# Two PSUM pools of four banks, another order of loads and of batch 0's work, and one two-term weight chunk in a fused attention and maxout kernel

## The chip, the cores and the metric

The kernel runs on one core of a Trainium2 chip. The metric is the time of one execution on the device in microseconds (us); lower is better. TensorE (PE in the profile, PEld for its weight loads) does the matmuls, VectorE (DVE), ScalarE (ACT) and GpSimd (POOL) do the casts, sums and copies, and SyncE's queue (SP) issues nearly all DMAs. Matmul results go to PSUM, which the kernel uses in banks of 128 x 512 fp32.

## The reference

```python
B, H, S, Ns, D = (8, 8, 512, 32, 64)          # n_tokens of the second part: B * (S + Ns)
scores = scale * x @ state.T ; a = softmax(scores)        # [B,H,S,Ns]
xread = a @ state                                         # [B,H,S,D]
scores2 = scale * state @ x.T ; a2 = softmax(scores2)
sread = a2 @ x                                            # [B,H,Ns,D]
t = concat([xread, sread], axis=2) -> [B * (S + Ns), H * D] = [4352, 512]
h1 = t @ w1 ; h2 = t @ w2                                 # d_ff = 1024
out = maximum(h1, h2) @ w_out                             # [4352, 512]
```

All inputs and the output are float32 in HBM.

## The kernel before, in words

**Algebra.** max(h1, h2) is h2 + relu(h1 - h2), so the kernel needs W1 - W2 (`wcat`, columns 0 to 1023) and W2 @ W_out (`wcat`, columns 1024 to 1535, made by `w_wo`). xread is a @ state, so for each batch the small matrix S W = blockdiag(state) @ wcat (`SW`, made by `u_sw` in chunks of 512 columns) takes the place of xread @ W. A batch of 512 tokens is then a first layer `l1` (eight tiles: a @ SW, then relu into `r`) and a second layer `l2` (four output tiles `c`: two matmuls for the linear part, eight for relu @ W_out).

**One batch's preparation.** `compact_x` (ScalarE) casts x to `xc`, `d_xt` transposes it by DMA to `xt`; `u_exp` makes the scores and their exponentials `e`; `u_norm` the row sums `es`, reciprocals `er` and products `a`; `d_at` transposes `a` by DMA to `aT` (in batches 0 and 1 `u_at` does it on TensorE). `u_sr` (lines 235 to 249) reads the same `e` for the other direction: 32 matmuls into one bank, from which VectorE takes a reciprocal `rr` and a product `sr`; `u_srt` transposes that into `sread_t`. `u_sw` (lines 275 to 291) puts out the matmuls of all its chunks first, two banks for each, and then their copies: VectorE takes g=0, ScalarE g=1.

**Order.** The schedule is written by hand: instructions go to each engine's queue in the order of the program, and each engine works its queue in order. For batches 1 to 7 (lines 522 to 533) `fillers(b)` hangs the preparation of batch b+1 between the tiles of batch b: the scores after the last first-layer tile (slot 7), `u_sr` and the compaction of x(b+2) after output tile 0 (slot 8), `d_at` after tile 1 (slot 9), `u_sw` with all three chunks after tile 2 (slot 10), `u_srt` after tile 3 (slot 11). Output tiles 0 and 2 are copied from PSUM by VectorE, 1 and 3 by ScalarE (`l2_close`). For batch 0 and the making of weights the order is spelled out in lines 443 to 520, with warm-up matmuls in the gaps.

**PSUM.** Until batch 0 is done there are two pools of four banks, `ps` for short-lived tiles and `acc` for output tiles and W2 @ W_out. `one_ring` (line 521) then closes both, and one ring of eight banks serves everything. A new tile takes a bank only when the readers of its last tile are done.

**Two terms.** W1 - W2 is made by GpSimd (`w_sub`, four parts). Chunks of `SW` that are wanted sooner, (0,0), (0,1) and (1,1) as (batch, chunk), are made in two terms instead: state @ bf16(W1) plus (-state) @ bf16(W2), with `w1b`, `w2b` and `sneg`.

**Loads.** SP issues, in this order: states of batches 0 to 2, x(0), W2 left half, W_out quarters 0 and 1, W2 right half, W_out quarters 2 and 3, W1 left and right half, x(1), states of batches 3 to 7, x(2).

Of the kernel before, what the change touches and what calls it, by code (L numbers as in the profile page):

```python
# [9 lines left out]
BF16 = mybir.dt.bfloat16  # L10
# [5 lines left out]
def kernel(  # L16
# [14 lines left out]
    nc = tc.nc  # L31
# [6 lines left out]
    NF = FF // 128  # L38
    scale = 1.0 / (D ** 0.5)
    assert D == 64 and Ns == 32 and S == 512 and H == 8 and DM == 512 and B % 4 == 0  # L40
    TWO = 2
    WC = FF + DM

    consts = ctx.enter_context(tc.tile_pool(name="consts", bufs=1))
# [3 lines left out]
    keep = ctx.enter_context(tc.tile_pool(name="keep", bufs=2))  # L48
    big = ctx.enter_context(tc.tile_pool(name="big", bufs=2))

    early = ctx.enter_context(ExitStack())
    pools = dict(ps=early.enter_context(tc.tile_pool(name="ps", bufs=4, space=bass.MemoryType.PSUM)),
                 acc=early.enter_context(tc.tile_pool(name="acc", bufs=4, space=bass.MemoryType.PSUM)))
    ctx.enter_context(tc.manual_schedule())

    def bank(dtype=F32, kind="ps"):
        return pools[kind].tile([128, 512 if dtype == F32 else 1024], dtype, tag="b", name=kind)

    def acc():
        return bank(kind="acc")  # L60

    def one_ring():
        early.close()
        pools["ps"] = pools["acc"] = ctx.enter_context(tc.tile_pool(name="ring", bufs=8, space=bass.MemoryType.PSUM))

    def copy(eng, o, i):
        if eng == "A":
            nc.scalar.copy(o, i)  # L68
        elif eng == "V":
            nc.vector.tensor_copy(o, i)  # L70
        else:
            nc.gpsimd.tensor_copy(o, i)  # L72

    def negate(eng, o, i):
        (nc.vector if eng == "V" else nc.gpsimd).tensor_scalar(o, i, scalar1=-1.0, scalar2=None, op0=ALU.mult)
# [8 lines left out]
    def load_x(b, parts=1):  # L84
        xf_t[b] = xio.tile([128, H, NC * D], F32, tag="xf", name="xf")
        for g in range(parts):
            nc.sync.dma_start(out=xf_t[b][:, g::parts, :], in_=x[b, g::parts].rearrange("h (p c) d -> p h (c d)", c=NC))
# [3 lines left out]
    def load_states(bs):  # L91
        nc.sync.dma_start(out=s_f[:, 2 * bs.start:2 * bs.stop],
                          in_=state[bs].rearrange("b (q h) n d -> (h n) (b q) d", q=2))

    first, rest = slice(0, 3), slice(3, 8)
    w2f = stage.tile([128, 4, FF], F32)
    w1f = stage.tile([128, 4, FF], F32)
    wof = stage.tile([128, NF, DM], F32)
# [1 line left out]
    def load_w(t, w, ch):  # L100
        cs = slice(ch * 512, (ch + 1) * 512)
        nc.sync.dma_start(out=t[:, :, cs], in_=w.rearrange("(i p) f -> p i f", p=128)[:, :, cs])  # L102
# [3 lines left out]
                          in_=moe_w_out.rearrange("(k p) n -> p k n", p=128)[:, 2 * q:2 * q + 2])  # L106

    load_states(first)
    load_x(0)
    for ch in range(2):  # L110
        load_w(w2f, moe_w2, ch)
        load_wo(2 * ch)
        load_wo(2 * ch + 1)
    load_w(w1f, moe_w1, 0)
    load_w(w1f, moe_w1, 1)
    load_x(1)
    load_states(slice(3, 8))
    load_x(2)

    ident = consts.tile([128, 128], BF16)  # L120
# [2 lines left out]
    make_identity(nc, ident)  # L123
    sbd = consts.tile([128, B, H, 2, Ns], BF16)
    nc.vector.memset(sbd, 0.0)
    sneg = consts.tile([128, TWO, 4, Ns], BF16)
    wo = consts.tile([128, NF, DM], BF16)
    wcat = consts.tile([128, 4, WC], BF16)
    w1b = stage.tile([128, 4, FF], BF16)
    w2b = stage.tile([128, 4, FF], BF16)  # L130
    w2t = stage.tile([128, 4, NF, 128], BF16)

    def warm_up(n):
        p = bank()
        for k in range(n):
            nc.tensor.matmul(p, warm[:, 0:128], warm, start=(k == 0), stop=(k == n - 1))  # L136
# [28 lines left out]
    def negate_states():  # L165
        for g in range(2):
            gs = slice(64 * g, 64 * g + 64)
            negate("V", sneg[gs], sbd[gs, 0:TWO, g::2, g, :])


    sread_t = consts.tile([128, 4, B * Ns], BF16)
# [63 lines left out]
    def u_sr(b):  # L235

        d = st[b]
        d["sr"] = at.tile([128, 2, D], BF16, tag="sr", name="sr")
        d["rr"] = at.tile([128, 2], F32, tag="rr", name="rr")
        p = bank()  # L240
        for g in range(2):
            for c in range(NC):
                for i in range(4):
                    nc.tensor.matmul(p[32 * i:32 * i + 32, g * 65:g * 65 + 65], d["e"][:, g, i, c, :],  # L244
                                     d["xp"][:, 2 * i + g, c, 0:65],
                                     start=(c == 0 and g == 0), stop=(c == NC - 1 and g == 1))
        pv = p[:, 0:130].rearrange("p (g u) -> p g u", g=2)
        nc.vector.reciprocal(d["rr"], p[:, 64:130:65])
        nc.vector.tensor_mul(d["sr"], pv[:, :, 0:64], d["rr"].unsqueeze(2).to_broadcast([128, 2, D]))
# [23 lines left out]
    swt = consts.tile([128, 2, 2, WC], BF16)  # L273

    def sw_mm(b, ch, engs="VA"):
        pg = [bank(), bank()]
        two = b < TWO and ch < 2 and (b, ch) != (1, 0)
        terms = ((sbd, w1b), (sneg, w2b)) if two else ((sbd, wcat),)
        for k, (sv, w) in enumerate(terms):
            for i in range(4):  # L280
                for g in range(2):
                    gs = slice(64 * g, 64 * g + 64)
                    nc.tensor.matmul(pg[g][32 * i:32 * i + 32, :],  # L283
                                     sneg[gs, b, i, :] if k else sbd[gs, b, 2 * i + g, g, :],
                                     w[gs, i, ch * 512:(ch + 1) * 512],
                                     start=(k == 0), stop=(k == len(terms) - 1))
        return lambda: [copy(engs[g], SW[b][:, g, ch * 512:(ch + 1) * 512], pg[g]) for g in range(2)]

    def u_sw(b, *chs):
        for out_of in [sw_mm(b, ch) for ch in chs]:  # L290
            out_of()
# [92 lines left out]
                nc.sync.dma_start(out=out[b * L + S:(b + 1) * L], in_=ob[32 * q:32 * q + 32, t, :])  # L384


    def w_sub(q):
        cs = slice(q * 256, (q + 1) * 256)
        nc.gpsimd.tensor_sub(wcat[:, :, cs], w1f[:, :, cs], w2f[:, :, cs])  # L389

    def w_cast(o, w, ch, engs="VA"):
        cs = slice(ch * 512, (ch + 1) * 512)
        for k in range(2):
            copy(engs[k], o[:, 2 * k:2 * k + 2, cs], w[:, 2 * k:2 * k + 2, cs])
# [16 lines left out]
    def w_wo(q, i):  # L411
        if q == 0:
            WO[i] = acc()
        for f in range(2 * q, 2 * q + 2):
            nc.tensor.matmul(WO[i], w2t[:, i, f, :], wo[:, f, :], start=(f == 0), stop=(f == NF - 1))  # L415
        if q == 3:
            copy("V" if i % 2 else "A", wcat[:, i, FF:WC], WO[i])


    def fillers(b):  # L420
        fill = {}

        def put(slot, *units):
            fill.setdefault(slot, []).extend(units)

        n = b + 1
        if n < B:
            put(7, lambda: u_sc(n, 0), lambda: u_sc(n, 1))
            put(8, lambda: u_sr(n))
        if n + 1 < B:  # L430
            put(8, lambda: compact_x(n + 1, 0), lambda: compact_x(n + 1, 1))
        if n < B:
            put(9, lambda: d_at(n))
            put(10, lambda: u_sw(n, 0, 1, 2))
        if n + 1 < B:
            put(10, lambda: d_xt(n + 1))
        if n < B:
            put(11, lambda: u_srt(n))
        return fill
# [3 lines left out]
    warm_up(6)  # L443
    cast_states("V", first)
    states(first)
    warm_up(5)
    cast_x(0, (("V", slice(0, 4, 2)), ("A", slice(4, 8, 2)), ("V", slice(1, 4, 2)), ("P", slice(5, 8, 2))))
    u_xt(0, 0, "V")
    u_xt(0, 1, "A")
    u_exp(0, 0)  # L450
    u_exp(0, 1)
    w_cast(w2b, w2f, 0, "VV")
    wo_cast(0, "P")
    wo_cast(1, "P")
    warm_up(1)
    w_t(0, 0, "A")
    w_t(0, 1, "A")
    u_norm(0, 0, nc.vector)
    u_sr(0)
    u_norm(0, 1, nc.vector)  # L460
    negate_states()
    warm_up(3)
    for q in range(2):
        for i in range(4):
            w_wo(q, i)
    w_cast(w2b, w2f, 1)
    wo_cast(2, "P")
    w_t(1, 0, "V")
    w_t(1, 1, "A")
    u_at(0, "V")  # L470
    u_srt(0)
    wo_cast(3, "V")
    for i in range(4):
        w_wo(2, i)
    w_cast(w1b, w1f, 0)
    w_sub(0)
    w_sub(1)
    for i in range(4):
        w_wo(3, i)
    u_sw(0, 0)  # L480
    u_sw(0, 2)
    l1(0, {}, range(0, 4))
    for c in range(NC):
        l2_open(0, c)
    w_cast(w1b, w1f, 1)
    compact_x(1, 0)
    compact_x(1, 1)
    d_xt(1)
    cast_x(1)
    w_sub(2)  # L490
    w_sub(3)
    cast_states("P", rest)
    load_x(3)
    sT = d_states(rest)
    l2_add(0, 0, range(0, 4))
    u_sw(0, 1)
    for c in range(1, NC):
        l2_add(0, c, range(0, 4))
    l1(0, {}, range(4, 8))
    u_sc(1, 0, nc.vector)  # L500
    u_sc(1, 1, nc.gpsimd)
    cast_x(2)
    l2_add(0, 0, range(4, 8))
    l2_close(0, 0)
    u_sw(1, 0)
    l2_add(0, 1, range(4, 8))
    l2_close(0, 1)
    u_sw(1, 1)
    u_sr(1)
    compact_x(2, 0)  # L510
    compact_x(2, 1)
    l2_add(0, 2, range(4, 8))
    l2_close(0, 2)
    u_at(1, "V")
    l2_add(0, 3, range(4, 8))
    l2_close(0, 3)
    d_xt(2)
    u_sw(1, 2)
    u_srt(1)
    l2_out(0)  # L520
    one_ring()
    for b in range(1, B):
        fill = fillers(b)
        if b + 2 < B:
# [39 lines left out]
```

The softmax here doesn't subtract the row's maximum and nothing guards it: scores larger than these inputs give would overflow.

## Time and profile before

| | |
|---|---|
| median of 8 runs | 152.27 us (151.82 to 153.05) |
| profiled execution | 152.10 us, span from first to last instruction 150.2 us |
| TensorE busy | 141.9 us (94%) |
| VectorE, ScalarE, GpSimd busy | 82.3, 75.7, 43.9 us |
| DMA | 29.89 MB, 199 GB/s over the span; 364 to 390 GB/s from 4 to 23 us |
| TensorE clock granted | 0.988 of full speed |
| first matmul of batch 1's first layer | 42.04 us |
| one batch from there (batches 1 to 6) | 13.96 us |

How to read it: a row of the timeline gives the start, the time from the first start to the last end, the engine, the line of the kernel, the operation, `out<-in`, and how often; a square bracket holds the idle time ahead of it and what ended that. Matmuls overlap: a 128x512 matmul is shown with 0.379 us, and the next starts 0.216 us after it. Rows of the chain of waits hold a start, a duration and what ran or was waited for; "issue" is time without a cause that the profile shows.

### The profile page before, as it was taken

How to read it: one execution, taken by the hardware profiler on the slowest of the kernel's cores; microseconds unless marked ns; L12 is line 12 of the kernel's file. 1: busy time of each engine (PE TensorE's matmuls, PEld its weight loads, DVE VectorE, ACT ScalarE, POOL GpSimd, SP SyncE). 2: the span in 40 equal slices, each digit the busy share in tenths (PEclk: the TensorE clock that was granted, in tenths of full speed). 3: DMA queues.
4: the chain of work that ended last, by engine and by line, in shares of the span. 5: the costliest groups of instructions: out<-in, count | busy, mean ns of one | idle time of the engine just before them, and what ended most of it. 6: DMA issues, size and time to landing. Idle time of an engine off the chain costs nothing.

```text
span 150.2 us, 3032 instructions
## 1 busy us (share of the span) xinstructions
PE 141.9 (94%) x1255; PEld 68.1 (45%) x1255; DVE 82.3 (55%) x151; ACT 75.7 (50%) x126; POOL 43.9 (29%) x44
## 2 busy tenths in 40 slices
PE   6859999999989999999999999999999999999990
PEld 1347553343435445444543444345445434764460
DVE  5368558428968187716854583658067725721120
ACT  3057239926869147717744683478157136521000
POOL 3025129995843430550064017104100500000000
PEclk9987999999999999999999999999999999999999
DMA  4999999988699877974979397951596030502423
GB/s 87 365 390 387 388 385 334 300 164 248 124 257 299 226 132 236 313 147 79 293 266 195 123 283 222 149 232 61 105 111 279 0 74 35 244 0 70 140 105 110
DMA packets 37934, 29.89 MB, mean 199 GB/s; under 512 B 24864, under 2 KB 33312, under 8 KB 37024
## 3 DMA queue, kind: packets, MB, share of 16 engines
q1 hardware_dynamic: 37776, 29.56, 70.1%
q8 instruction: 10, 0.16, 0.5%
q10 hardware_dynamic: 144, 0.13, 0.3%
q14 instruction: 4, 0.03, 0.1%
HBM read 15.20 MB, written 8.91 MB: 161 GB/s over the span
## 4 chain that ended last, share of the span: by engine, by line
PE 71%; DMA 13%; SPq 8%; ACT 3%; DVE 2%; issue 1%
PE acc L326 32%; PE ps L311 16%; DMA xf<-in_x_dram 10%; PE acc L322 9%; SPq L102 4%; SPq L105 3%; PE ps L283 3%; DMA xt<-xc 3%; PE ps L370 2%; PE acc L380 2%; PE ps L221 2%; PE acc L360 1%; PE ps L244 1%; ACT xc L68 1%; PE acc L378 1%; DVE es L228 1%
## 5 line engine op out<-in xcount | busy, mean ns | idle before, releaser
L326 PE MATMUL acc<-wo,r 128*128 128x512 bf16 x248 | 58.9, 379 | 0.0
L326 PEld LDWEIGHTS <-r 128*128 128x128 bf16 x248 | 23.9, 98 | 28.8 <-issue 0.6
L301 DVE TENSOR_SCALAR r<-ps 128x512 bf16<-128x512 f32 x32 | 22.1, 692 | 16.2 <-PE ps L311 16.1
L311 PE MATMUL ps<-aT,swt 128*128 128x512 bf16 x128 | 29.1, 379 | 0.9 <-ACT sread_t L68 0.8
L231 POOL TENSOR_TENSOR a<-e,er 128x512 bf16<-128x512 bf16 x13 | 13.4, 1048 | 54.2 <-ACT e L224 27.2
L70 DVE COPY ob<-acc 128x512 f32<-128x512 f32 (+1 forms) x17 | 11.1, 653 | 30.1 <-PE acc L326 29.7
L68 ACT COPY ob<-acc 128x512 f32<-128x512 f32 (+1 forms) x16 | 9.2, 573 | 28.6 <-PE acc L326 21.0
L299 ACT ACTIVATE r<-ps 128x512 bf16<-128x512 f32 x32 | 19.2, 601 | 8.3 <-PE ps L311 7.7
L68 ACT CAST swt<-ps 128x512 bf16<-128x512 f32 x24 | 12.9, 593 | 12.3 <-PE ps L283 12.2
L311 PEld LDWEIGHTS <-swt 128*128 128x128 bf16 x128 | 12.1, 98 | 15.3 <-DVE swt L70 1.3
L322 PE MATMUL acc<-swt,aT 128*128 128x512 bf16 x62 | 18.1, 381 | 0.0
L72 POOL CAST xp<-xf 128x2048 bf16<-128x2048 f32 (+1 forms) x8 | 14.1, 1768 | 10.6 <-DMA xf<-in_x_dram 10.6
L70 DVE CAST swt<-ps 128x512 bf16<-128x512 f32 x24 | 15.3, 682 | 1.7 <-PE ps L283 1.7
L68 ACT CAST xc<-xf 128x1024 bf16<-128x1024 f32 x14 | 14.0, 1051 | 0.1
L228 DVE TENSOR_REDUCE es<-e 128x16 f32<-128x512 bf16 x16 | 10.6, 662 | 1.8 <-ACT e L224 1.8
L389 POOL TENSOR_TENSOR wcat<-w1f,w2f 128x1024 bf16<-128x1024 f32 x4 | 9.8, 2475 | 2.9 <-DMA w1f<-in_moe_w_dram 2.9
L224 ACT ACTIVATE e<-ps 128x512 bf16<-128x512 f32 x16 | 8.8, 595 | 1.3 <-PE ps L221 0.6
L136 PE MATMUL ps<-warm 128*128 128x512 bf16 x15 | 6.3, 568 | 1.3 <-POOL warm L122 1.3
L322 PEld LDWEIGHTS <-aT 128*128 128x128 bf16 x62 | 4.7, 98 | 6.0 <-issue 2.6
L415 PE MATMUL acc<-wo,w2t 128*128 128x512 bf16 x32 | 7.2, 379 | 0.0
L283 PE MATMUL ps<-wcat,sbd 64*32 64x512 bf16 x168 | 6.7, 380 | 0.1
L221 PEld LDWEIGHTS <-xt 128*128 128x128 bf16 x128 | 5.0, 101 | 2.9 <-ACT xt L68 0.7
(68 smaller groups left out, 104.4 us busy)
## 6 DMA issues: line engine op xcount, KB each, us to landing
xf<-in_x_dram SPq DMA_DIRECT2D x8, 1024.0 KB, 7.6
out_dram<-ob SPq DMA_DIRECT2D x7, 1024.0 KB, 5.0
w2f<-in_moe_w_dram SPq DMA_DIRECT2D x2, 1024.0 KB, 10.4
wof<-in_moe_w_out_dram SPq DMA_DIRECT2D x4, 512.0 KB, 11.4
w1f<-in_moe_w_dram SPq DMA_DIRECT2D x2, 1024.0 KB, 15.0
out_dram<-ob SPq DMA_DIRECT2D x3, 256.0 KB, 2.7
out_dram<-obs SPq DMA_DIRECT2D x8, 64.0 KB, 1.7
s_f<-in_state_dram SPq DMA_DIRECT2D x1, 320.0 KB, 13.7
```

The source lines that it names most:

```text
L68: nc.scalar.copy(o, i)
L70: nc.vector.tensor_copy(o, i)
L72: nc.gpsimd.tensor_copy(o, i)
L228: nc.vector.tensor_reduce(d["es"][:, g], d["e"][:, g].rearrange("p i c n -> p (i c) n"), axis=mybir.AxisListType.X, op=ALU.add)
L231: mul.tensor_mul(d["a"][:, g].rearrange("p c i n -> p i c n"), d["e"][:, g], d["er"][:, g].rearrange("p (i c) -> p i c", i=4).unsqueeze(3) ...
L283: nc.tensor.matmul(pg[g][32 * i:32 * i + 32, :], sneg[gs, b, i, :] if k else sbd[gs, b, 2 * i + g, g, :], w[gs, i, ch * 512:(ch + 1) * 512 ...
L299: nc.scalar.activation(out=o, in_=p, func=ACTF.Relu)
L301: nc.vector.tensor_scalar(o, p, scalar1=0.0, scalar2=None, op0=ALU.max)
L311: nc.tensor.matmul(p, SW[b][:, g, f * 128:(f + 1) * 128], AT[b][:, g, :], start=(g == 0), stop=(g == 1))
L322: nc.tensor.matmul(OB[b][1 + c], AT[b][:, g, c * 128:(c + 1) * 128], SW[b][:, g, FF:WC], start=(g == 0), stop=False)
L326: nc.tensor.matmul(OB[b][1 + c], R[b][:, f, c * 128:(c + 1) * 128], wo[:, f, :], start=False, stop=(f == NF - 1))
L389: nc.gpsimd.tensor_sub(wcat[:, :, cs], w1f[:, :, cs], w2f[:, :, cs])
```

## The change

It does these things at once:

- The two PSUM pools of four banks stay for the whole kernel. `u_sw` takes `acc` banks for its third chunk from batch 2 on, `ps` banks otherwise.
- In the steady loop `u_sr(n)` goes from slot 8 to slot 10, directly ahead of `u_sw(n)`.
- Only chunk (0,0) has two terms. `w_sub` parts 2 and 3 go from GpSimd to VectorE, `w1b` has half the columns and is cast in three parts by VectorE, ScalarE and GpSimd.
- States of batch 0 alone lead the queue of loads; those of batches 1 and 2 come just before x(1), are cast by GpSimd and transposed on TensorE within batch 0's second layer. x(0) is loaded in two halves (even and odd heads).
- Early casts go to other engines, and there are 25 warm-up matmuls instead of 15.
- Batch 0's second layer: `u_sw(1,0)` moves ahead of the scores of batch 1, both of batch 1's products `a` go to GpSimd, and three of the four copies of output tiles move behind the last tile.

```diff
-    early = ctx.enter_context(ExitStack())
-    pools = dict(ps=early.enter_context(tc.tile_pool(name="ps", bufs=4, space=bass.MemoryType.PSUM)),
-                 acc=early.enter_context(tc.tile_pool(name="acc", bufs=4, space=bass.MemoryType.PSUM)))
+    pools = {k: ctx.enter_context(tc.tile_pool(name=k, bufs=4, space=bass.MemoryType.PSUM)) for k in ("ps", "acc")}
...
-    first, rest = slice(0, 3), slice(3, 8)
+    first, second, rest = slice(0, 1), slice(1, 3), slice(3, 8)
...
     load_states(first)
-    load_x(0)
+    load_x(0, 2)
...
     load_w(w1f, moe_w1, 1)
+    load_states(second)
     load_x(1)
...
     def sw_mm(b, ch, engs="VA"):
-        pg = [bank(), bank()]
-        two = b < TWO and ch < 2 and (b, ch) != (1, 0)
+        pg = [bank(kind="acc" if ch == 2 and b > 1 else "ps") for g in range(2)]
+        two = (b, ch) == (0, 0)
...
-    def w_sub(q):
+    def w_sub(q, eng=nc.gpsimd):
         cs = slice(q * 256, (q + 1) * 256)
-        nc.gpsimd.tensor_sub(wcat[:, :, cs], w1f[:, :, cs], w2f[:, :, cs])
+        eng.tensor_sub(wcat[:, :, cs], w1f[:, :, cs], w2f[:, :, cs])
...
             put(7, lambda: u_sc(n, 0), lambda: u_sc(n, 1))
-            put(8, lambda: u_sr(n))
...
-            put(10, lambda: u_sw(n, 0, 1, 2))
+            put(10, lambda: u_sr(n), lambda: u_sw(n, 0, 1, 2))
...
-    warm_up(5)
-    cast_x(0, (("V", slice(0, 4, 2)), ("A", slice(4, 8, 2)), ("V", slice(1, 4, 2)), ("P", slice(5, 8, 2))))
+    warm_up(9)
+    cast_x(0, (("A", slice(0, 4, 2)), ("V", slice(4, 8, 2)), ("P", slice(1, 4, 2)), ("V", slice(5, 8, 2))))
...
-    w_cast(w2b, w2f, 0, "VV")
+    w_cast(w2b, w2f, 0, "PA")
...
-    w_cast(w1b, w1f, 0)
+    for e, i in (("V", slice(0, 2)), ("A", slice(2, 3)), ("P", slice(3, 4))):
+        copy(e, w1b[:, i, 0:512], w1f[:, i, 0:512])
...
     l1(0, {}, range(0, 4))
-    for c in range(NC):
-        l2_open(0, c)
-    w_cast(w1b, w1f, 1)
+    w_sub(2, nc.vector)
+    w_sub(3, nc.vector)
     compact_x(1, 0)
     compact_x(1, 1)
     d_xt(1)
+    cast_states("P", second)
+    cast_states("P", rest)
     cast_x(1)
-    w_sub(2)
-    w_sub(3)
-    cast_states("P", rest)
     load_x(3)
     sT = d_states(rest)
+    for c in range(NC):
+        l2_open(0, c)
     l2_add(0, 0, range(0, 4))
+    l2_add(0, 1, range(0, 4))
+    states(second)
+    l2_add(0, 2, range(0, 4))
     u_sw(0, 1)
-    for c in range(1, NC):
-        l2_add(0, c, range(0, 4))
+    l2_add(0, 3, range(0, 4))
     l1(0, {}, range(4, 8))
-    u_sc(1, 0, nc.vector)
-    u_sc(1, 1, nc.gpsimd)
+    u_sw(1, 0)
+    u_exp(1, 0)
+    u_exp(1, 1)
+    u_norm(1, 0, nc.gpsimd)
+    u_norm(1, 1, nc.gpsimd)
     cast_x(2)
     l2_add(0, 0, range(4, 8))
-    l2_close(0, 0)
-    u_sw(1, 0)
+    u_sw(1, 1)
+    u_sr(1)
     l2_add(0, 1, range(4, 8))
     l2_close(0, 1)
-    u_sw(1, 1)
-    u_sr(1)
     compact_x(2, 0)
     compact_x(2, 1)
+    d_xt(2)
     l2_add(0, 2, range(4, 8))
-    l2_close(0, 2)
+    u_sw(1, 2)
     u_at(1, "V")
-    l2_add(0, 3, range(4, 8))
-    l2_close(0, 3)
-    d_xt(2)
-    u_sw(1, 2)
+    l2_add(0, 3, range(4, 6))
     u_srt(1)
+    l2_add(0, 3, range(6, 8))
+    for c in (3, 0, 2):
+        l2_close(0, c)
     l2_out(0)
-    one_ring()
```

More of the change, by code (lines that the diff above doesn't have):

```diff
@@ L40 @@
     assert D == 64 and Ns == 32 and S == 512 and H == 8 and DM == 512 and B % 4 == 0
-    TWO = 2
     WC = FF + DM
@@ L60, in acc @@
         return bank(kind="acc")
-    def one_ring():
-        early.close()
-        pools["ps"] = pools["acc"] = ctx.enter_context(tc.tile_pool(name="ring", bufs=8, space=bass.MemoryType.PSUM))
     def copy(eng, o, i):
@@ L115 @@
     load_w(w1f, moe_w1, 1)
+    load_states(second)
     load_x(1)
-    load_states(slice(3, 8))
+    load_states(rest)
     load_x(2)
@@ L125 @@
     nc.vector.memset(sbd, 0.0)
-    sneg = consts.tile([128, TWO, 4, Ns], BF16)
+    sneg = consts.tile([128, 4, Ns], BF16)
     wo = consts.tile([128, NF, DM], BF16)
     wcat = consts.tile([128, 4, WC], BF16)
-    w1b = stage.tile([128, 4, FF], BF16)
+    w1b = stage.tile([128, 4, 512], BF16)
     w2b = stage.tile([128, 4, FF], BF16)
@@ L167, in negate_states @@
             gs = slice(64 * g, 64 * g + 64)
-            negate("V", sneg[gs], sbd[gs, 0:TWO, g::2, g, :])
+            negate("V", sneg[gs], sbd[gs, 0, g::2, g, :])
     sread_t = consts.tile([128, 4, B * Ns], BF16)
@@ L283, in sw_mm @@
                     nc.tensor.matmul(pg[g][32 * i:32 * i + 32, :],
-                                     sneg[gs, b, i, :] if k else sbd[gs, b, 2 * i + g, g, :],
+                                     sneg[gs, i, :] if k else sbd[gs, b, 2 * i + g, g, :],
                                      w[gs, i, ch * 512:(ch + 1) * 512],
@@ L415, in w_wo, with w_wo_out @@
             nc.tensor.matmul(WO[i], w2t[:, i, f, :], wo[:, f, :], start=(f == 0), stop=(f == NF - 1))
-        if q == 3:
-            copy("V" if i % 2 else "A", wcat[:, i, FF:WC], WO[i])
+    def w_wo_out(i):
+        copy("V" if i % 2 else "A", wcat[:, i, FF:WC], WO[i])
     def fillers(b):
@@ L445 @@
     states(first)
-    warm_up(5)
-    cast_x(0, (("V", slice(0, 4, 2)), ("A", slice(4, 8, 2)), ("V", slice(1, 4, 2)), ("P", slice(5, 8, 2))))
+    warm_up(9)
+    cast_x(0, (("A", slice(0, 4, 2)), ("V", slice(4, 8, 2)), ("P", slice(1, 4, 2)), ("V", slice(5, 8, 2))))
     u_xt(0, 0, "V")
+    warm_up(2)
     u_xt(0, 1, "A")
     u_exp(0, 0)
+    warm_up(2)
     u_exp(0, 1)
-    w_cast(w2b, w2f, 0, "VV")
+    warm_up(3)
+    w_cast(w2b, w2f, 0, "PA")
+    u_norm(0, 0, nc.vector)
+    u_norm(0, 1, nc.vector)
+    w_t(0, 0, "A")
+    w_t(0, 1, "A")
+    u_sr(0)
     wo_cast(0, "P")
@@ L455 @@
     warm_up(1)
[L456 to L465, printed above, removed]
+    for i in range(4):
+        w_wo(0, i)
+    u_at(0, "V")
     w_cast(w2b, w2f, 1)
-    wo_cast(2, "P")
+    for i in range(4):
+        w_wo(1, i)
     w_t(1, 0, "V")
     w_t(1, 1, "A")
-    u_at(0, "V")
+    negate_states()
+    wo_cast(2, "P")
+    wo_cast(3, "P")
     u_srt(0)
-    wo_cast(3, "V")
+    warm_up(2)
     for i in range(4):
         w_wo(2, i)
-    w_cast(w1b, w1f, 0)
+    for e, i in (("V", slice(0, 2)), ("A", slice(2, 3)), ("P", slice(3, 4))):
+        copy(e, w1b[:, i, 0:512], w1f[:, i, 0:512])
+    for i in range(4):
+        w_wo(3, i)
+    for i in range(4):
+        w_wo_out(i)
+    u_sw(0, 0)
+    u_sw(0, 2)
     w_sub(0)
     w_sub(1)
[L478 to L481, printed above, removed]
     l1(0, {}, range(0, 4))
-    for c in range(NC):
-        l2_open(0, c)
-    w_cast(w1b, w1f, 1)
+    w_sub(2, nc.vector)
+    w_sub(3, nc.vector)
     compact_x(1, 0)
```

## The prediction

> **What bounds the kernel now.** I read the page first, then the table of busy time by stage, the chain of waits that ended last, and the timelines of TensorE and VectorE around one batch. The stage table (us from the start, TensorE, weight loads, VectorE, ScalarE, GpSimd, clock, DMA share, GB/s):
>
> ```profile
> 0.00:22.20 22.20, 18.58 (x171) 10.35 (x172) 13.22 (x23) 8.17 (x10) 5.41 (x12) 0.92 0.94 333
> ...
> 34.30:42.04 7.74, 6.68 (x106) 3.01 (x106) 7.06 (x14) 6.15 (x11) 5.30 (x7) 1.00 0.78 191
> 42.04:146.80 104.76, 104.71 (x896) 50.27 (x896) 55.33 (x104) 52.20 (x93) 21.58 (x21) 1.00 0.64 168
> ```
>
> From 42.04 us (batch 1's first layer) to 146.80 TensorE has no gap. The other engines are half idle there, so only TensorE's own work, or a new wait in its queue, moves that part. Ahead of it the chain is one of loads:
>
> ```profile
> 12.78 15.17 DMA xf<-in_x_dram
> 27.94 0.02 issue
> 27.97 1.99 ACT xc L68 x2
> 29.96 0.03 ACT swt L68
> 29.99 4.36 DMA xt<-xc
> 34.34 0.04 issue
> 34.39 0.42 PE ps L221 x8
> ...
> 42.04 3.62 PE ps L311 x16
> 45.66 0.47 PE ps L221 x16
> ```
>
> x of batch 1 lands at 27.94, ScalarE compacts it, the DMA transposes it, and batch 1's scores start at 34.39. So whatever is gained before 27.94 on other tiles is lost again in waiting for this load. From 34.39 to 42.04 a chain through VectorE and ScalarE holds TensorE back, and the stage has 7.74 - 6.68 = 1.06 us of TensorE gaps. Batches 1 to 6 then take 13.96 us each (first layers at 42.04, then 56.17, 70.13, 84.09).
>
> [...] VectorE starts the next instruction 0.60 us after the 0.69 us copy at 48.33, in program order. [...] GpSimd's same subtraction took 2.34 to 2.86 us. [...] the stage with gaps of 1.06 us in all ran at 1.00.
>
> **The change, part by part.**
>
> *(a) Pools of four, and u_sr moved.* From batch 1 on, u_sr(n) leaves its place after the first output tile and stands directly ahead of u_sw(n), after the third. Its bank is now one of four. In the built program u_sw's second chunk takes for g=1 the bank that u_sr wrote a moment before, in each of batches n = 2 to 7, and its weight load waits for VectorE. VectorE's queue is: copy of the third output tile (ob), reciprocal rr, product sr. The product frees the bank. The rows of the same group today:
>
> ```profile
> 48.22 0.44 PE L244 MATMUL ps<-xp,e 128*32 128x65 bf16 x32
> 48.59 0.61 PE L322 MATMUL acc<-swt,aT 128*128 128x512 bf16 x2
> ...
> 53.01 0.84 PE L283 MATMUL ps<-wcat,sbd 64*32 64x512 bf16 x24
> ```
>
> ```profile
> 48.33 0.69 DVE L70 COPY ob<-acc 128x512 f32<-128x512 f32 x1
> 48.93 0.16 DVE L248 RECIPROCAL rr<-ps 128x2 f32<-128x2 f32 x1
> 49.13 0.29 DVE L249 TENSOR_TENSOR sr<-ps,rr 128x128 bf16<-128x128 f32 x1
> 53.12 0.69 DVE L70 COPY ob<-acc 128x512 f32<-128x512 f32 x1 [3.70 <-PE acc L326]
> ```
>
> The first group is the second layer's first tile: u_sr follows it at 48.22, and VectorE ends sr at 49.13 + 0.29 = 49.42, 1.20 after. Nothing waits for that today. Moved behind the third tile it has the same three VectorE steps behind it (that tile's copy starts at 53.12, 0.11 after the matmuls that follow, as at 48.33). So: u_sr starts at 0, u_sw's first chunk at 0.37 (48.59 - 48.22), eight matmuls of 0.77/24 = 0.032 take 0.26, one more 0.03: at 0.66 TensorE wants the bank. It is free at 1.20 plus 0.04 for the release (the chain's "issue" steps are 0.02 to 0.04) = 1.24. Wait: 0.58 us. Six batches: 3.5 us, all on the path, since TensorE has no gap that could take it in. Not shown by any row is how a release in mid-group is paid: low end 0.45 (the product's bank counted free at its issue end, the next VectorE step starting 0.1 before the end of the one ahead), high end 0.70 [...]. I take 0.58. Behind the waiting matmul stand the rest of u_sw and the fourth tile; the swt copies follow 0.5 later, but have the fourth tile (0.43 + 1.73) as cover, and the next first layer needs only part of them at its start. The other rings of four hold: a first-layer tile takes 0.43, its bank comes back after 0.17 + 0.69, and is wanted after three others, 1.29.
>
> *(b) Loads.* States of batches 1 and 2 (128 KB) move from the front to just before x(1), and x(0) comes in two halves. At the page's 385 GB/s everything up to W1 comes 0.34 us sooner, but the bytes ahead of x(1) are the same: it lands at 27.9 again. SP issues two more DMAs (some 0.5 us each by the rows of its queue); its next urgent one, the transposition at 29.99, has 4.2 us of slack behind x(2), issued by 25.79. Zero. If x(1) landed later, every tenth would go straight to the end.
>
> *(c) W1 cast by three engines, two-term chunks fewer.* W1a's cast ends some 0.3 sooner (0.60 and 0.69 for ScalarE's and VectorE's parts, 1.05 before for ScalarE's); two chunks lose their eight second-term matmuls each, 2 x 0.26 = 0.5 us of TensorE. Both lie ahead of 34.39 or inside a stretch with gaps. VectorE gets two subtractions, [...] u_sw(0,1) wants them at 30.8. If they took GpSimd's 2.35 each, 31.7: 0.9 late, of which the 0.3 us that TensorE has left before 34.39 takes a part, cost 0.6. Walking TensorE's new order from the first layer of batch 0 (about 24.45): 1.73 + 1.73 + 3 x 0.87 + 0.3 (states) + 0.34 + 0.87 + 1.73 + 0.34 = 9.65, that is 34.1. So scores at 34.39 as before. The casts dealt anew ahead of 22 us (w2b's first half to GpSimd and ScalarE, W_out's last quarter from VectorE's 0.68 to GpSimd's 1.04) hide behind the wait for W1, which ends at 22.2; uncovered they cost 0.4 each. Ten more warm-up matmuls lie in waits for loads ahead of 22 us: zero; uncovered, 10 x 0.22 = 2.2.
>
> *(d) Batch 0's second layer and closes.* From 34.87 TensorE runs tile 0 (0.95), u_sw(1,1) 0.34, u_sr 0.37, tile 1 and 2 (0.93 each), u_sw(1,2) 0.34, and meets u_at at 38.7. Both products now come from GpSimd: VectorE's sums start at 35.47 and a pair ends 3.17 later (46.56 to 49.73 in batch 2's rows), 38.64: in time. Then 0.5 + 0.45 + 0.06 + 0.45: batch 1's first layer at 40.15 instead of 42.04. The copies (VectorE tiles 0 and 2, ScalarE 3) lie behind it. But batch 2's x is late next: ScalarE's compaction stands behind the copy of tile 1, whose matmuls end at 37.6, so it runs 38.1 to 40.1 (38.34 to 40.33 before), and with 4.36 for the transposition xt(2) is there at 44.5. The first layer would end at 43.7. So batch 2's scores start at 44.5 instead of 45.50: gain 1.0, not 1.9. Ends: 1.8 if the transposition takes less, a loss of 0.2 if it takes the 5.7 that its slowest issue took.
>
> **The sum** against the profiled execution (152.10 us: span 150.2 and 1.9 around it): + 3.5 - 1.0 = 154.6. The runs' median is 152.27, 0.17 above it: 154.8.
>
> **The rivals.**
> 1. *The start gives nothing.* xt(2) or x(1) comes later by what (d) gains (two small loads more in SP's queue, or a transposition of 5.1, still within what the trace allows), or the subtractions are slow. For: the start hangs on DMA times. Against: their order is nearly the same. 152.27 + 3.5 = 155.8.
> 2. *The bank wait is short* (the other side). One mechanism: u_sr's bank is free by the time TensorE comes to it, since VectorE's three steps overlap u_sr and the first chunk more than the rows say. It decides at 1.0/6 = 0.17 us per batch: below that the start's gain wins. At 0.08 each: 152.27 - 1.0 + 0.5 = 151.8. For: the ends of TensorE's matmuls are modelled. Against: the copy ahead takes 0.6 on its own and can't start before the tile ends; rr and sr need another 0.5.
>
> **How the numbers follow.** Forecast (154.8, with 153.2 to 156.0 as its own range, from 6 x 0.45 - 1.8 and 6 x 0.70 - 0.5): 0.64. Rival 1: 0.24. Rival 2: 0.12, of which 0.08 is faster by over 0.3% and 0.04 within it (0.3%, or 0.46 us, is about what a measurement of this kernel tells from no change). The range takes the first two: 153.2 to 156.2.
>
> **What would show it.** Right: six gaps of TensorE, 0.5 to 0.7 us each, between the eighth and the tenth matmul of u_sw, ended by VectorE's sr (line 243 of the new kernel), batches of about 14.5 us instead of 13.96; first layer of batch 1 near 40.2; a gap ahead of batch 2's scores, ended by the transposition. Wrong: batches of 13.96; scores of batch 1 other than at 34.4; other gaps between 34 and 44 us.

## The result and the profile after

The changed kernel takes 154.70 us (median of 11 runs, 154.52 to 155.03) against 152.27: 1.0161 times as long (95% interval 1.0142 to 1.0180), slower by 2.4 us. Its profiled execution has a span of 152.8 us against 150.2.

The stage table's last long row in the changed kernel, from batch 2's scores at 44.85 almost to the end (columns as in the table of before):

```profile
44.85:149.50 104.65, 102.92 (x880) 49.23 (x880) 52.74 (x101) 50.39 (x88) 20.13 (x20) 1.00 0.57 160
```

From batch 2's scores to the end TensorE now shows 104.65 - 102.92 = 1.73 us of gaps where it showed 0.05 in before's long row, all of one kind; the clock granted is 1.00 in both rows. The chain of waits through one of them, in batch 1:

```profile
50.24 1.74 PE acc L322 x8
51.98 0.02 issue
52.01 0.69 DVE ob L63
52.70 0.09 DVE rr L242
52.79 0.02 issue
52.81 0.30 DVE sr L243
53.11 0.04 issue
53.16 0.41 PE ps L279 x7
```

Output tile 2 ends at 51.98; VectorE copies it, then makes the reciprocal and the product sr; only then does u_sw (L279) go on. The list of waits has it six times, once for each of batches n = 2 to 7, both for the weight loads and for the matmuls behind them (total us, times, longest):

```profile
PE ps L279 <- DVE sr L243: 1.7, 6, 0.3
PEld L279 <- DVE sr L243: 4.6, 6, 0.8
```

Neither is what TensorE loses. Where the first nine matmuls start at 52.27, their weight loads are over at 52.38 and the next one starts 0.78 later, at 53.16. The matmuls show less: the nine are drawn to 52.87, 0.29 ahead of the tenth, since one is drawn with 0.386 us in the mean while the step from one to the next is 0.032 (24 in 0.77 in the kernel before). What TensorE loses is read from the batches: first layers start at 56.10, 70.62, 85.15, 99.67, 114.20, 128.72, so one takes 14.52 us instead of 13.96. Six times 0.56 is + 3.4. The chain of the start:

```profile
34.78 0.64 PE ps L215 x16
...
38.48 2.00 ACT xc L61 x2
40.48 0.03 ACT swt L61
40.50 4.31 DMA xt<-xc
44.81 0.05 issue
44.85 0.64 PE ps L215 x16
```

Batch 1's first layer starts at 40.57 (42.04 before), but batch 2's scores wait for x(2)'s transposition and start at 44.85 (45.50 before): - 0.65. From the last first layer to the end it is 24.08 us instead of 24.23. Together 3.4 - 0.65 - 0.15 = 2.6, the difference of the spans; the 0.15 at the end was not looked into.

### The profile page after: what moved, and what is told of

It is laid out like the page before. It is cut to its first block, busy times and chain, and to the rows that moved or that the text cites. A ratio compares the mean times of both kernels' runs of the same rounds, so it can differ in the third digit from the quotient of the medians.

```text
span 152.8 us, 3015 instructions
## 1 busy us (share of the span) xinstructions
PE 143.1 (94%) x1249; PEld 67.9 (44%) x1249; DVE 83.0 (54%) x150; ACT 75.5 (49%) x126; POOL 44.4 (29%) x47
## 4 chain that ended last, share of the span: by engine, by line
PE 72%; DMA 13%; DVE 6%; SPq 3%; ACT 2%; issue 1%
PE acc L322 34%; PE ps L307 16%; DMA w1f<-in_moe_w_dram 10%; PE acc L318 9%; DMA xt<-xc 3%; DVE ob L63 3%; PE ps L215 2%; PE ps L279 2%; PE ps L366 2%; PE acc L376 2%; SPq L98 2%; PE acc L356 1%; ACT xc L61 1%; DVE sr L243 1%; PE acc L374 1%
## 5 line engine op out<-in xcount | busy, mean ns | idle before, releaser
L225 POOL TENSOR_TENSOR a<-e,er 128x512 bf16<-128x512 bf16 x14 | 14.4, 1048 | 49.7 <-ACT e L218 34.2
L61 ACT CAST swt<-ps 128x512 bf16<-128x512 f32 x18 | 10.5, 586 | 17.8 <-PE ps L279 17.8
L63 DVE CAST swt<-ps 128x512 bf16<-128x512 f32 x18 | 11.8, 684 | 0.9 <-PE ps L279 0.9
L279 PE MATMUL ps<-wcat,sbd 64*32 64x512 bf16 x136 | 8.6, 386 | 1.7 <-DVE sr L243 1.7
L130 PE MATMUL ps<-warm 128*128 128x512 bf16 x25 | 8.0, 446 | 1.3 <-POOL warm L116 1.3
L318 PEld LDWEIGHTS <-aT 128*128 128x128 bf16 x62 | 5.2, 98 | 7.0 <-issue 2.5
L215 PE MATMUL ps<-sbd,xt 128*128 128x64 bf16 x128 | 5.2, 193 | 1.7 <-ACT swt L61 0.7
```

The lines of the kernel that those rows point to most:

```text
L215: nc.tensor.matmul(p[:, k * 64:k * 64 + 64], d["xt"][:, 4 * i + 2 * g + cp, :], sbd[:, b, 2 * i + g].rearrange("p u n -> p (u n)"), start= ...
L225: mul.tensor_mul(d["a"][:, g].rearrange("p c i n -> p i c n"), d["e"][:, g], d["er"][:, g].rearrange("p (i c) -> p i c", i=4).unsqueeze(3) ...
L279: nc.tensor.matmul(pg[g][32 * i:32 * i + 32, :], sneg[gs, i, :] if k else sbd[gs, b, 2 * i + g, g, :], w[gs, i, ch * 512:(ch + 1) * 512], ...
L318: nc.tensor.matmul(OB[b][1 + c], AT[b][:, g, c * 128:(c + 1) * 128], SW[b][:, g, FF:WC], start=(g == 0), stop=False)
```

## The experiments

Eleven kernels, in three groups, each against the kernel before on the same chip. Its medians there were 152.58 (sr_slot8, sr_acc, before_steady, sw_021), 152.28 (ring8, c2_act, xc_early, s2_act) and 152.18 (before_move, st_late, best); differences of that size, 0.4 us, between kernels of different groups are not read from medians. "Batch" is the mean from the second first layer of the loop to the last in the profile, "scores 2" the start of batch 2's scores.

| kernel | median us | ratio to before (95% interval) | batch us | scores 2 |
|---|---|---|---|---|
| before | 152.27 | | 13.96 | 45.50 |
| changed | 154.70 | 1.0161 (1.0142 to 1.0180) | 14.52 | 44.85 |
| sr_slot8 | 151.33 | 0.9934 (0.9909 to 0.9959) | 13.96 | 44.97 |
| sr_acc | 150.74 | 0.9886 (0.9853 to 0.9919) | 13.85 | 45.07 |
| ring8 | 150.95 | 0.9895 (0.9829 to 0.9961) | 13.85 | 45.03 |
| before_steady | 155.18 | 1.0208 (1.0149 to 1.0267) | 14.53 | 45.33 |
| sw_021 | 153.27 | 1.0059 (1.0037 to 1.0081) | 14.31 | 45.02 |
| c2_act | 153.45 | 1.0076 (1.0059 to 1.0093) | 14.32 | 44.94 |
| before_move | 151.56 | 0.9955 (0.9941 to 0.9970) | 13.85 | 46.07 |
| xc_early | 155.06 | 1.0157 (1.0096 to 1.0218) | 14.53 | 44.76 |
| st_late | 153.79 | 1.0099 (1.0065 to 1.0132) | 14.52 | 43.86 |
| s2_act | 154.69 | 1.0139 (1.0083 to 1.0195) | 14.52 | 45.13 |
| best | 149.74 | 0.9837 (0.9787 to 0.9887) | 13.85 | 44.07 |

**sr_slot8: u_sr back in its old place.**

```diff
             put(7, lambda: u_sc(n, 0), lambda: u_sc(n, 1))
+            put(8, lambda: u_sr(n))
...
-            put(10, lambda: u_sr(n), lambda: u_sw(n, 0, 1, 2))
+            put(10, lambda: u_sw(n, 0, 1, 2))
```

> The changed kernel with one edit undone: u_sr stands again in slot 8, after the first output tile; pools of four stay. Theory (u_sw's second chunk waits for u_sr's bank only because u_sr stands just ahead of it): batches of 13.96 us again, no wait of a weight load on the product sr, 154.7 - 6 x 0.565 = 151.3 us. Rival A (two pools of four are too few in the loop wherever u_sr stands): still near 14.5 us a batch, 154.7. Rival B (the start is the cost, not the loop): 154.7 as well, with batches as they were.

151.33 us, batches of 13.96, and the wait for sr is gone from the list. Pools of four alone cost nothing in the loop, and what is left of the change is a gain: the loop was the whole loss.

**sr_acc: u_sr's bank from the other pool.**

```diff
 def u_sr(b):
...
-        p = bank()
+        p = bank(kind="acc" if b > 1 else "ps")
```

> The changed kernel with one edit: from batch 2 on u_sr takes its bank from the acc pool; it stays in slot 10, directly ahead of u_sw. Theory (it is the bank, not the place nor the later sums on VectorE): u_sw goes through, batches of 13.96 us (up to 14.05 if output tile 3 now meets a bank late), 151.3 to 151.8 us. Rival (the place in slot 10 itself costs, since VectorE's copies of swt start 0.4 us later): batches stay above 14.3, 153.5 or more.

150.74 us. The group in batch 2 of this kernel, TensorE and VectorE:

```profile
65.97 0.44 PE L238 MATMUL acc<-xp,e 128*32 128x65 bf16 x32
...
66.34 0.63 PE L279 MATMUL ps<-wcat,sbd 64*32 64x512 bf16 x16
...
66.78 0.40 PE L279 MATMUL acc<-wcat,sbd 64*32 64x512 bf16 x8
...
66.89 0.29 DVE L243 TENSOR_TENSOR sr<-acc,rr 128x128 bf16<-128x128 f32 x1
```

VectorE ends sr at 67.18, as late as in the changed kernel (1.21 after u_sr's start), but u_sw runs through from 66.34. So it is neither the place of u_sr nor VectorE's later copies, but one bank. The batch of 13.85 us is below the 13.96 that the theory gave; before_move goes into that.

**ring8: one ring of eight banks after batch 0, u_sr still in slot 10.**

```diff
-    pools = {k: ctx.enter_context(tc.tile_pool(name=k, bufs=4, space=bass.MemoryType.PSUM)) for k in ("ps", "acc")}
+    early = ctx.enter_context(ExitStack())
+    pools = {k: early.enter_context(tc.tile_pool(name=k, bufs=4, space=bass.MemoryType.PSUM)) for k in ("ps", "acc")}
...
+    def one_ring():
+        early.close()
+        pools["ps"] = pools["acc"] = ctx.enter_context(tc.tile_pool(name="ring", bufs=8, space=bass.MemoryType.PSUM))
...
     l2_out(0)
+    one_ring()
```

> The changed kernel with one edit undone: after batch 0 the two pools are closed and one ring of eight banks serves all, as before the change; u_sr stays in slot 10. Theory: with eight banks the one that u_sr wrote is not among the next six, no wait, batches of 13.96 us, 151.3 us. So neither the move nor the pools alone costs, only both. Rival (the place of u_sr costs by itself): batches above 14.3, 153.5 or more.

150.95 us, 13.85 a batch. The move costs only together with the pools of four, the pools only together with the move. The ring has a price of its own at the start: batch 1's first layer begins at 41.57, where it begins between 40.39 and 40.84 in the other kernels with the new start, and what it waits for is VectorE's copies of batch 0's output tiles:

```profile
41.57 3.63 PE L312 MATMUL ps<-aT,swt 128*128 128x512 bf16 x16 [1.13 <-DVE ob L68]
```

It stays hidden: batch 2's scores, which start at 45.03 here, start between 44.76 and 45.13 in all kernels with the new start whose transposition of x(2) keeps its place behind that of sT.

**before_steady: the loop's part alone, on the kernel before.**

```diff
-        pg = [bank(), bank()]
+        pg = [bank(kind="acc" if ch == 2 and b > 1 else "ps") for g in range(2)]
...
-            put(8, lambda: u_sr(n))
...
-            put(10, lambda: u_sw(n, 0, 1, 2))
+            put(10, lambda: u_sr(n), lambda: u_sw(n, 0, 1, 2))
...
-    one_ring()
```

> The kernel before with only the loop's part of the change: pools of four to the end, u_sr in slot 10, u_sw's third chunk in acc banks from batch 2 on. Start, loads and casts as before. Theory (loop + 3.4, start - 0.65 to - 1): 152.27 + 3.4 = 155.7 us, batches of 14.53, scores of batch 2 at 45.5. Rival (the new start costs and the loop does less than thought): 154 or less.

155.18 us, 2.6 above the median of before on that chip; by the interval of the ratio it is 2.3 to 4.1 us slower, which takes in the 3.4 expected. The profile is sharper: 14.53 a batch, with the old start.

**sw_021: eight matmuls more ahead of the bank.**

```diff
-            put(10, lambda: u_sr(n), lambda: u_sw(n, 0, 1, 2))
+            put(10, lambda: u_sr(n), lambda: u_sw(n, 0, 2, 1))
```

> The changed kernel with u_sw's chunks in the order 0, 2, 1 in the loop. Chunk 2 has acc banks, so eight more matmuls (0.26 us) run before the bank of u_sr is wanted. Theory (a wait for a fixed moment, VectorE's end of sr): each wait shrinks by 0.26, from 0.565 to 0.31, batches of 14.27, 154.7 - 6 x 0.26 = 153.2 us. Rival (a fixed cost of restarting TensorE or of the bank change): no smaller, 154.7.

153.27 us, 14.31 a batch: the cost falls by 0.21 of the 0.26 that the eight matmuls take. It is a wait for a moment, not a fixed price.

**c2_act: output tile 2 copied by ScalarE.**

```diff
-        copy("A" if c % 2 else "V", ob[:, c, :], OB[b][1 + c])
+        copy("A" if c % 2 or (c == 2 and b > 0) else "V", ob[:, c, :], OB[b][1 + c])
```

> The changed kernel with the copy of output tile 2 on ScalarE instead of VectorE in the loop (batches 1 to 7). Then VectorE's reciprocal need not wait for that copy (0.60 us) but only for u_sr's last matmul, about 0.45 us after the start of u_sr. Theory: sr ends some 0.2 us sooner, each wait falls from 0.57 to about 0.35, 154.7 - 6 x 0.2 = 153.5 us; ScalarE's copies of swt start 0.5 later, covered by output tile 3. Rival (the copy ahead is the whole of the wait): down to nothing, 151.3. Rival (ScalarE is then late with swt or with the bank of tile 2): no gain, 154.7 or more.

153.45 us, 14.32 a batch. In batch 2 VectorE starts the reciprocal 0.50 us after the start of u_sr (66.80 - 66.30), where it was 0.72 in the changed kernel (52.62 - 51.90):

```profile
66.30 0.44 PE L238 MATMUL ps<-xp,e 128*32 128x65 bf16 x32
...
66.80 0.17 DVE L242 RECIPROCAL rr<-ps 128x2 f32<-128x2 f32 x1 [3.99 <-PE acc L322]
...
67.01 0.29 DVE L243 TENSOR_TENSOR sr<-ps,rr 128x128 bf16<-128x128 f32 x1
...
67.35 0.14 PEld L279 LDWEIGHTS <-sbd 64*32 64x32 bf16 x15 [0.57 <-DVE sr L243]
```

Some two thirds of the wait (14.32 - 13.85 = 0.47 of 0.67 a batch) stay without the copy ahead: u_sr's own matmuls, the reciprocal and the product. The bracket on the reciprocal names the matmuls of the output tile, which ended long before it; it was u_sr's end, at 66.74.

**before_move: only u_sr in slot 10, ring of eight.**

```diff
-            put(8, lambda: u_sr(n))
...
-            put(10, lambda: u_sw(n, 0, 1, 2))
+            put(10, lambda: u_sr(n), lambda: u_sw(n, 0, 1, 2))
```

> The kernel before with one edit: u_sr in slot 10, directly ahead of u_sw; the ring of eight banks stays. Theory (TensorE loses about 0.1 us where a stream of 128x512 matmuls gives way to a group of small ones, and u_sr and u_sw side by side make one such place of two): batches of 13.85 instead of 13.96 us, 152.3 - 6 x 0.107 = 151.6 us. Rival (the 13.85 us of the runs with acc bank and with eight banks comes from the new start or the pools): 13.96, 152.3.

151.56 us, 13.85 a batch: the move by itself is a gain of 0.11 per batch. The same stretch of TensorE in the kernel before and then in this one:

```profile
60.36 1.89 PE L326 MATMUL acc<-wo,r 128*128 128x512 bf16 x8
62.18 0.43 PE L244 MATMUL ps<-xp,e 128*32 128x65 bf16 x32
...
65.15 1.89 PE L326 MATMUL acc<-wo,r 128*128 128x512 bf16 x8
66.97 0.84 PE L283 MATMUL ps<-wcat,sbd 64*32 64x512 bf16 x24
```

```profile
60.82 1.89 PE L326 MATMUL acc<-wo,r 128*128 128x512 bf16 x8
62.55 0.59 PE L322 MATMUL acc<-swt,aT 128*128 128x512 bf16 x2
...
65.14 1.89 PE L326 MATMUL acc<-wo,r 128*128 128x512 bf16 x8
66.96 0.43 PE L244 MATMUL ps<-xp,e 128*32 128x65 bf16 x32
67.32 0.84 PE L283 MATMUL ps<-wcat,sbd 64*32 64x512 bf16 x24
```

Eight matmuls take 1.73 from start to start when 128x512 matmuls follow (60.82 to 62.55), and 1.82 when a group of small ones does (60.36 to 62.18, 65.15 to 66.97). From u_sr to u_sw there is no such step (66.96 to 67.32 is u_sr's own 0.36). Side by side the two groups pay it once.

**xc_early: x(2) compacted ahead of the copy of tile 1.**

```diff
     l2_add(0, 1, range(4, 8))
-    l2_close(0, 1)
     compact_x(2, 0)
     compact_x(2, 1)
     d_xt(2)
+    l2_close(0, 1)
```

> The changed kernel with x(2)'s compaction on ScalarE ahead of the copy of batch 0's output tile 1 instead of behind it. In the changed kernel batch 2's scores wait 0.67 us for the transposition of x(2), which starts when the compaction ends at 40.48. Theory (this chain sets the start): the compaction begins up to 0.7 us sooner, batch 2's scores at about 44.2 instead of 44.85, 154.1 us. Rival (TensorE or the banks of batch 1's first layer are late as well): no gain, 154.7.

155.06 us: no gain. The theory fell in this form. SP's queue issued the transposition 1.2 us sooner (39.31 instead of 40.50), but the issue took 3.00 us instead of 1.83 and batch 2's scores hardly moved:

```profile
39.31 3.00 SPq L189 DMA_TRANSPOSE xt<-xc  x1
...
44.76 0.64 PE L215 MATMUL ps<-sbd,xt 128*128 128x64 bf16 x16 [0.47 <-DMA xt<-xc]
```

**st_late: the edit of xc_early, and sT's transposition behind x(2)'s.**

```diff
-    sT = d_states(rest)
...
-    l2_close(0, 1)
     compact_x(2, 0)
     compact_x(2, 1)
     d_xt(2)
+    sT = d_states(rest)
+    l2_close(0, 1)
```

> The changed kernel with x(2)'s compaction ahead of the copy of tile 1 (as in xc_early) and with the transposition of the states of batches 3 to 7 (sT) issued behind that of x(2) instead of ahead of it. In xc_early x(2)'s transposition was issued 1.2 us sooner (39.31 instead of 40.50), its issue took 3.0 instead of 1.8 us and batch 2's scores came only 0.1 us sooner. Theory (the transpositions and the load of x(3) share the DMA engines, and sT's, 4.1 us at issue, is in the way): scores at 44.1 to 44.3, where the first layer ends, so 154.0 to 154.2 us. Rival (x(3)'s megabyte or something else holds it): scores near 44.8, 154.7.

153.79 us. Scores at 43.86, right behind the first layer, which began at 40.39:

```profile
39.04 2.12 SPq L189 DMA_TRANSPOSE xt<-xc  x1
...
43.86 0.63 PE L215 MATMUL ps<-sbd,xt 128*128 128x64 bf16 x16
```

TensorE does not wait for x(2) any more. Of the 0.90 by which the scores come sooner than in xc_early, 0.27 belongs to the two executions, since batch 1's scores and x(2)'s issue are already 0.27 sooner (34.60 and 39.04 against 34.87 and 39.31); the rest, 0.63, is what the order of the two transpositions gave at least. The runs say the same: 153.65 to 153.94 us, where xc_early took 154.48 to 155.35. Between xc_early and this kernel only sT's transposition moved, so it is what held x(2)'s: starting x(2)'s sooner helped only with sT's out of its way. The trace's own figure for the landing of x(2)'s transposition here, 6.2 us after its issue, lies behind the scores that read it and is not used. By what means (its place in the queue, or transfers under way at the same time) was not taken apart further.

**s2_act: the states of batches 1 and 2 cast by ScalarE.**

```diff
+    cast_states("A", second)
     compact_x(1, 0)
...
-    cast_states("P", second)
```

> The changed kernel with the cast of batch 1's and 2's states on ScalarE, ahead of x(1)'s compaction, instead of GpSimd. In the changed kernel VectorE's two subtractions took 1.68 us each [...], and GpSimd's cast of those states 1.61 for 512 elements while its cast of 1280 took 1.25 in the kernel before. Theory (the two engines hold each other up when both work on SBUF at once): with GpSimd idle from about 27.4 to 29.4 [...] the time does not move (154.7 within 0.3), since the cover held. Rival (1.68 is the price of such a subtraction with this layout): both stay near 1.65.

154.69 us, no move, as expected. VectorE's two subtractions and GpSimd's rows beside them, first in the changed kernel, then in this one:

```profile
22.75 4.66 POOL L385 TENSOR_TENSOR wcat<-w1f,w2f 128x1024 bf16<-128x1024 f32 x2
26.76 3.29 DVE L385 TENSOR_TENSOR wcat<-w1f,w2f 128x1024 bf16<-128x1024 f32 x2
27.35 1.61 POOL L65 CAST s_bf<-s_f 128x512 bf16<-128x512 f32 x1
29.43 1.73 POOL L65 CAST s_bf<-s_f 128x1280 bf16<-128x1280 f32 x1 [0.46 <-DMA s_f<-in_state_dram]
```

```profile
22.86 4.66 POOL L385 TENSOR_TENSOR wcat<-w1f,w2f 128x1024 bf16<-128x1024 f32 x2
26.86 2.88 DVE L385 TENSOR_TENSOR wcat<-w1f,w2f 128x1024 bf16<-128x1024 f32 x2
29.54 1.30 POOL L65 CAST s_bf<-s_f 128x1280 bf16<-128x1280 f32 x1 [2.02 <-DMA s_f<-in_state_dram]
```

The second subtraction, counted from the end of the first, took 3.29 - 1.74 = 1.55 beside GpSimd's casts and 2.88 - 1.75 = 1.13 here, with GpSimd idle until 29.54, 0.2 us before its end: it fell, as the theory has it. The first did not get shorter: it took 1.75 here and 1.74 in the changed kernel, although GpSimd was idle for the last 1.09 us of it here. So what counts is not how long both work at once. The rows fit the two engines taking turns instead. GpSimd's own subtraction, which was under way when VectorE's first began, ended at 27.41 in the changed kernel and at 27.52 here, and VectorE's first ended 1.09 after that in both (28.50 and 28.61). In the changed kernel VectorE's second ended 1.09 after GpSimd's cast of 512 elements (30.05 after 28.96), and GpSimd's cast of 1280 ended 1.11 after VectorE's second (31.16 after 30.05), near the 1.30 that the whole cast took here and the 1.25 in the kernel before. This is read from two traces, in which GpSimd's spans are rough; no run was made to test it. Either way the subtraction's own price is 1.09 to 1.13 us in these two runs. The rest of the 1.55 to 1.75 goes with GpSimd's work beside it.

**best: sr_acc and st_late together.**

> The changed kernel with u_sr's bank from the acc pool from batch 2 on (as in sr_acc) and the two edits of st_late. Theory: the sum of both, 150.7 to 150.8 of sr_acc less what st_late gains (0.6 if its theory holds), 150.1 us; 150.7 if the start's edits give nothing.

149.74 us, 0.9837 of before (0.9787 to 0.9887): below both kernels. It keeps the changed start with st_late's two edits, gives u_sr an acc bank, and has scores 2 at 44.07.

## Why the prediction held, point by point

The forecast was 154.8 us and the median is 154.70. The two mechanisms were the right ones; that the sum came so close is in part luck, because four misses nearly cancel: the bank wait cost 0.5 us more than forecast over six batches (0.67 instead of 0.58 each), a gain of 0.6 in the loop was not foreseen, the start gave 0.35 less, and 0.15 at the end is unexplained.

- *What bounds:* right. The loop had no slack for a wait in TensorE's queue, and the start was held by x(1)'s load and the transpositions.
- *(a), the bank wait:* the mechanism, its place and its six occurrences were right, and the size near: + 3.4 against 3.5. But two errors met in it. The wait costs 14.52 - 13.85 = 0.67 per batch, not 0.58, near the high end of 0.70, which was my estimate and not shown by a row. By starts it is 0.60 (u_sw's tenth matmul would have started at 51.90 + 0.37 + 0.26 + 0.03 = 52.56 and did at 53.16), and the fifteen matmuls behind it took 0.55 to the next group instead of 0.49. Against that stands a gain that the prediction had not seen: u_sr and u_sw side by side save 0.11 (before_move). That a waiting matmul holds everything behind it shows as well: the eight matmuls of u_sw's third chunk have acc banks and yet start behind the tenth matmul, at 53.18; put ahead of it in sw_021 they run through.
- *(b), loads:* x(1) landed in time for a compaction at 28.00 (27.97 before): zero, as said. Batch 1's scores came at 34.78, not 34.39, because this time its transposition took 4.7 us, until about 34.7. The chain of waits names ScalarE's copy swt there, which ended within 0.05 of it; the matmul's bank had been free since a relu that ended at 33.91, and the weight load's row names the transposition. Both starts have it: 34.39, 34.84 and 34.97 in the three kernels with the old one, 34.58 to 35.05 in the others. I had taken one execution's 4.36 us for the value.
- *(c), casts and subtractions:* hidden, as said. VectorE's two subtractions, 1.68 us each, ran from 26.76 to 30.05, against the 30.58 at which u_sw(0,1) began: 0.5 of cover left. That VectorE would be so much quicker than GpSimd's 2.35 was my estimate; no row of before showed it. What was dealt anew ahead of 22 us cost nothing: W1's cast began at 21.62 (22.25 before). One thing there the prediction did not look at: the clock granted from 0 to 22.2 us is 1.00 in the changed kernel's profile, with ten more warm-up matmuls, and 0.92 in that of before, where it was 0.51 from 10 to 12 us and 0.63 from 12 to 14. Over the whole span it was 0.996 to 1.000 in every execution with the new start, and 0.973 to 1.000 in those with the old one. Which part of the new start raised it was not taken apart, and no time was gained that the wait for x(1) did not take back.
- *(d), batch 0's second layer:* gain 0.65 instead of 1.0. "Batch 2's x is late next" was right, with the compaction at 38.48 (38.1 predicted), the transposition's 4.31 (4.36) and scores at 44.85 (44.5): the miss is the 0.39 by which batch 1's scores came later. Of the 1.47 us by which batch 1's first layer came sooner (40.57 instead of 42.04), 0.65 was left at batch 2's scores; the rest went into the wait for x(2). (The prediction's bad end has a slip: 40.1 + 5.7 is 45.8, a loss of 0.3 and not 0.2.)
- *Rival 1* (no gain at the start) is out: sr_slot8, with the old loop, is 0.66% below before (0.41% to 0.91%). *Rival 2* (a wait below 0.17) is out.

## What to carry to other kernels

When a small group of matmuls is moved next to another, ask which buffer the second takes and who has to free it: with few banks it may be the one that the first has just filled, and then the reader's whole queue, here a copy, a reciprocal and a product, comes to stand in TensorE's path (here 14.52 us a batch against 13.85 with a bank of the other pool). The loss was one bank, not the design: another pool for one tile turned a loss of 1.6% into a gain of 1.1%. And a gain in front of a transfer lasts only until the next transfer (here 0.65 us was left of 1.47): look for what is late next before counting it.

## What the runs showed of the hardware that was not expected

- TensorE lost 0.09 us where 128x512 matmuls gave way to small ones (1.82 instead of 1.73 us for eight), and nothing from u_sr to u_sw (66.96 to 67.32, u_sr's own 0.36); the batch in before_move is 0.11 shorter.
- VectorE's fp32 subtraction of 1024 elements took 1.55 to 1.75 us where GpSimd was at work when its turn came (three times, in the changed kernel and s2_act), and 1.13 where GpSimd was idle until 0.2 us before its end (s2_act); in the three it ended 1.09 us after GpSimd's instruction did. GpSimd's cast of 1280 elements took 1.73 with 0.62 us of it beside a subtraction, 1.30 with 0.2 beside one (s2_act) and 1.25 in the kernel before.
- A DMA transposition issued 1.2 us sooner (39.31 instead of 40.50) fed TensorE 0.1 us sooner while another transposition was ahead of it in the queue; with that one moved behind it, scores came 0.9 us sooner (43.86 instead of 44.76), at least 0.6 of it by the order.
- The clock granted to TensorE in the first 22.2 us was 1.00 in the changed kernel's profile, with ten more warm-up matmuls, and 0.92 in that of before; over the whole span it was 0.996 to 1.000 in the executions with the new start and 0.973 to 1.000 in those with the old one. What raised it was not taken apart.
